# A new order of loads, and first weight products quarter by quarter, in a planned attention and feed-forward kernel

## The chip, the cores and the metric

The kernel runs on one core of a Trainium2 chip. The metric is the device time in microseconds (us) of one execution. Before the change the median of three runs is 355.5 us (355.44 to 355.51). The profiled execution took 354.98 us, and the instructions in its trace span 353.2 us; all moments below count from the start of that span.

## The reference

`q`, `k`, `v` have the shape (8 batches, 12 heads, 448 positions, 64). The reference computes

```python
q_n, k_n = rmsnorm(q, g_q), rmsnorm(k, g_k)
scores = q_n @ k_n.T / 8
attn = exp(scores - max); attn = attn / sum(attn)
x = (attn @ v)            # heads side by side: 3584 tokens x 768
a = x @ w1; b = x @ w2    # 768 -> 1024
out = ((a * b) @ w3) @ w_out   # 1024 -> 1024 -> 768
```

Inputs and output are float32.

## The kernel before, in words

**Tiling.** Attention is done in 24 "quads" of four heads each: quad `i` is batch `i // 3`, heads `4 * (i % 3)` onward. A quad needs its q and k (448 KB each in SBUF), a preparation (`plan_prep`: square on ACT, row sums on DVE, two short ACT instructions for the inverse root, scaling on DVE, then a transpose), seven score steps (`do_score`: four matmuls into two PSUM banks, then one exponential of 128x896 on ACT, 0.92 us), and the product of the exponentials with v (`do_pv_main`, `do_pv_rest`), which also sums them. Up to quad 4 (`N_PE_T = 5`) the transpose is done by TensorE (`do_turn`), later by a DMA. Two quads, when both are ready, go through the value product together: 72 long matmuls and 24 short ones.

**Weights.** Since nothing stands between `w3` and `w_out`, the kernel first makes their product `w34s`. For that, eight row blocks of `w3` (`load_w3`, called w0 to w7 in the load order) are turned over by TensorE (`do_w3_turn`, eight 128x128 transposes and a copy into `w3T`), and eight pairs of PSUM banks (`w34_pair`) each sum 64 matmuls over the eight row blocks of `w_out`, which come in four loads (`load_wout`, o0 to o3). `w1` and `w2` come in three loads each (a0 to a2, b0 to b2). Each batch then has eight `ffn1_pair`s (48 matmuls each: a, b and their product on DVE), and each two batches seven `ffn2_pair`s (64 matmuls each). These pairs of sums are the filler: TensorE works on them whenever no score or value product is ready.

**Halves of a pair.** A pair fills two banks. All contributions of one bank first come in one assignment of the array's row halves, then the halves change over. Before the change-over a "hand-over" instruction that does nothing (`hand_over`, L841) must pass on another queue, SyncE's until all of `w2` has landed and GpSimd's afterwards. `PARTS` says after which `w_out` row blocks the first three `w34_pair`s change over: `(4, 8)` means once in the middle of row blocks 0 to 3 and once in the middle of 4 to 7.

**The order of the work is planned in Python.** When the program is built, `Planner.run` plays the whole kernel through with fixed costs: each engine takes the job that can start first, and `pe_step` chooses TensorE's next piece. The instructions are written out in that order, and each engine's order is fixed from then on: an instruction whose data comes later than planned holds up all that stands behind it on its engine. The planner thinks of a load as an amount of work in a queue (the `moves` number, in us); two queues, SyncE's and GpSimd's, share the DMA engines, and a load lands `AFTER = 0.7` us after its last byte, and after 75 us of the plan `LATE` later still.

**What the names of the change mean.** `POOL_ORDER` is the order in which GpSimd issues its loads; `vN` and `qN` are v, and q with k, of quad N. `STOCK` and `PACE`: when at least `STOCK` feed-forward pairs wait, scores are started no closer than 1.7 us. `HOLD`: when set, a value product of two quads isn't started while pairs are unfinished and no waiting pair is ready. `quiet` in `plan_load_v`: from quad 4 on, the four v loads of a quad are issued only while less than `QUIET = 0.5` us of work is left in SyncE's queue. Where nothing else is ready in the first 13 us, TensorE is given matmuls on zeros (`do_warm`, L1182).

Of the kernel before, what the change touches and what calls it, by code (L numbers as in the profile page):

```python
# [19 lines left out]
INF = float("inf")  # L20
# [4 lines left out]
LAG = {"ACT": 0.11, "DVE": 0.09, "SP": 0.0, "POOL": 0.0}  # L25
AHEAD = {"SP": 2.0, "POOL": 1.6}
AFTER = 0.7
LATE = 1.0
BUSY = 75.0


# [14 lines left out]
class Planner:  # L46
# [11 lines left out]
    def add(self, *args, **kw):  # L58
        self.jobs.append(Job(*args, **kw))
# [37 lines left out]
    def commit(self, job, start, engine):  # L97
# [9 lines left out]
        if job.moves is not None:  # L107
# [4 lines left out]
            def landed(t):  # L112
                self.note(job, t, engine)
                t += LATE if t > BUSY else 0.0
                ticket[0] = t
# [80 lines left out]
def kernel(  # L196
# [48 lines left out]
    MARGIN = 0.25  # L245
    LOW = 2
    PV_BANKS = 6
    HOLD = 1
    SOON = 0
    STARVED = 4  # L250
    HUNGRY = 0.6
    ONE = 0
    PARTS = ((4, 8), (4, 8), (4, 8))
    EARLY_PAIRS = 3
    AHEAD_W3 = 4
    EARLY = 4
    STOCK = 18
    PACE = 1.7
    POOL_ORDER = (
        "w0 o0 o1 w1 w2 o2 o3 q1 v0 w3 w4 q2 v1 a0 w5 w6 a1 v2 w7 v3 q3 a2 q4 b0 b1 q5 b2".split()  # L260
    )
    ON_POOL = (1, 2, 3, 4, 5)
    IN_PARTS = (6, 7, 8)
    QUIET = 0.5

    w1s = const.tile([128, CM, DFF], BF, name="w1s")
# [47 lines left out]
    plan = Planner()  # L314
# [17 lines left out]
    w_at = {"w3": [INF] * CF, "w3T": [INF] * CF, "w_out": [INF] * 4, "w1": [INF] * NQB, "w2": [INF] * NQB}  # L332
# [6 lines left out]
    def all_of(times, n):  # L339
        return max(times) if len(times) == n else INF  # L340

    def put(where, key):
        def done(t):
            where[key] = t

        return done
# [23 lines left out]
    def plan_load_qk(i, key=None):  # L370
        eng, queue = (nc.gpsimd, "POOL") if i in ON_POOL else (nc.sync, "SP")
        parts = 2 if i in IN_PARTS else 1
        for which in range(2):
            got = []

            def done(t, which=which, got=got):
                got.append(t)
                landed[i]["qk"[which]] = all_of(got, parts)

            for n in range(parts):  # L380
                x0, x1 = 2 * n // parts, 2 * (n + 1) // parts
                add(
                    queue, {"SP": 0.4, "POOL": 0.75}[queue],
                    (QUAD * i - 30 if key is None else key) + which * 0.01 + n * 0.001,
                    lambda which=which, x0=x0, x1=x1: load_qk(i, which, eng, x0, x1),
                    needs=[lambda: qk_free[i % 3] + (1.0 if i > 5 else 0.0)],
                    done=done, moves=(1.4 / parts, 0.086),
                )

    def load_v(i, z):  # L390
# [15 lines left out]
    def plan_load_v(i, key):  # L406
        got = []

        def done(t):
            got.append(t)  # L410
            if len(got) == 4:
                landed[i]["v"] = max(got)

        def quiet():

            late = i <= 3 or next_score[0] >= i * NU - 3
            return 0.0 if late or sum(x[1] for x in plan.moving["SP"]) < QUIET else INF

        for z in range(4):
            add(  # L420
                "POOL", 0.62, key + z * 0.01, lambda z=z: load_v(i, z),
                needs=[lambda: v_free[i % 4] + (3.0 if i > 3 else 0.0), quiet], done=done,
                moves=((0.48, 0.06), (0.40, 0.05))[z % 2],
            )

    def load_w12(dst, src, m):
        return nc.gpsimd.dma_start(
            out=dst[:, 2 * m : 2 * m + 2, :].rearrange("p a f -> p (a f)"),
            in_=src.rearrange("(m p a) f -> m p (a f)", m=NQB, a=2)[m],
        )  # L430

    def load_w3(c):
        return nc.gpsimd.dma_start(
            out=w3s[:, c, :],
            in_=moe_w3.rearrange("(c p) f -> p c f", p=128)[:, c, :],
        )

    def load_wout(c):
        return nc.gpsimd.dma_start(
            out=w_outs[:, 2 * c : 2 * c + 2, :],  # L440
            in_=moe_w_out.rearrange("(c p) n -> p c n", p=128)[:, 2 * c : 2 * c + 2],
        )
# [194 lines left out]
    def score_ready(t):  # L637
# [6 lines left out]
        stock = sum(p.name != "w" for p in waiting)  # L644
        if stock >= STOCK and t < last_score[0] + PACE:
            return False
# [122 lines left out]
    def pv_summed(i, kind, z, end):  # L769
# [34 lines left out]
        if kind == 2:  # L804
            pv_end[i] = v_free[i % 4] = end + 0.2
            if i + 4 < NQ:
                plan_load_v(i + 4, -1.0)
# [85 lines left out]
    def w34_pair(fc):  # L893
        def evacuate(p, at):
# [23 lines left out]
            (side(0), side(1)), evacuate,  # L918
            PARTS[fc] if fc < len(PARTS) else None,
        )  # L920
# [309 lines left out]
    def pe_try(t, r):  # L1230
# [7 lines left out]
        if mode[0] == "v" and len(idle) >= 1 and size == 1:  # L1238
            return start_pv(t, 1, idle)
        last = HOLD and pairs and not any(p.ready() <= r for p in waiting)  # L1240
        if size == 2 and len(idle) >= PV_BANKS and not last:
# [45 lines left out]
    with tc.manual_schedule():  # L1287
        nc.vector.memset(warm_t, 0.0)
        nc.vector.memset(eps_t, 64e-6)
        nc.vector.memset(ones, 1.0)  # L1290
        nc.vector.memset(ones[HP:NP, 1], 0.0)
        nc.vector.memset(ones[0:HP, 2], 0.0)
        nc.vector.memset(ones_row, 1.0)
        for which in range(2):
            load_qk(0, which, nc.sync, 0, 1)
            load_qk(0, which, nc.scalar, 1, 2)
        nc.scalar.dma_start(out=g_row[:, 0], in_=g_q.unsqueeze(0))
        nc.scalar.dma_start(out=g_row[:, 1], in_=g_k.unsqueeze(0))
        nc.scalar.preload_act_table_set("natural_log_exp_and_others")
        make_identity(nc, ident)  # L1300
        for t_sb in v_bufs:
            nc.gpsimd.memset(t_sb[:, :, NF, :], 0.0)  # L1302
        def warm(n):
            for _ in range(n):
                nc.tensor.matmul(
                    out=ps_all[:, 7, :], lhsT=warm_t[:, 0:128], rhs=warm_t,
                    start=True, stop=True,
                )

        def g_product():  # L1310
            nc.vector.scalar_tensor_tensor(
                out=gp_row,
                in0=g_row[:, 0].unsqueeze(1).broadcast_to([1, 2, D]),
                scalar=8.0,
                in1=g_row[:, 1].unsqueeze(1).broadcast_to([1, 2, D]),
                op0=MULT, op1=MULT,
            )
            nc.tensor.matmul(
                out=ps_all[:, 6, 0:D], lhsT=ones_row, rhs=gp_row[:, 0],
                start=True, stop=True,  # L1320
            )
            nc.tensor.matmul(
                out=ps_all[:, 6, D : D + 1],
                lhsT=gp_row.rearrange("a x d -> a (x d)"), rhs=ones_row[:, 0:1],
                start=True, stop=True,
            )
            warm(1)

        def spread():
            nc.vector.tensor_copy(out=g_b, in_=ps_all[:, 6, 0:D])  # L1330
            nc.vector.tensor_copy(out=g_col, in_=ps_all[:, 6, D : D + 1])

        warm(WARM)
        free.update(ACT=4.0, DVE=4.0, SP=4.0, POOL=2.3, PE=7.2)
        plan.now = plan.moved_to = 2.2
        plan.moving["SP"].append([2.3, 2.6, lambda t: None, 0.086])
        landed[0].update(q=4.5, k=5.4)
        bank_at[6] = INF
        add(
            "DVE", 0.13, -13.0, g_product, needs=[lambda: 5.8], done=put(consts_at, "gp")  # L1340
        )
        add(
            "DVE", 0.22, -11.0, spread, needs=[lambda: consts_at["gp"] + 0.6],
            done=lambda t: consts_at.update(g=t + SEM) or bank_at.__setitem__(6, t + SEM),
        )
        for i in range(3):
            plan_prep(i)

        seq = [0]

        def weight(emit, moves, done):
            add("POOL", 0.6, -100.0 + seq[0], emit, done=done, moves=moves)

        for name in POOL_ORDER:
            what, x = name[0], int(name[1])
            seq[0] += 1
            if what == "o":
                weight(lambda x=x: load_wout(x), (2.15, 0.135), put(w_at["w_out"], x))
            elif what == "w":
                weight(lambda x=x: load_w3(x), (1.38, 0.172), put(w_at["w3"], x))  # L1360
            elif what == "v":
                plan_load_v(x, -100.0 + seq[0])
            elif what == "q":
                plan_load_qk(x, -100.0 + seq[0])
            else:
                dst, src, key = (w1s, moe_w1, "w1") if what == "a" else (w2s, moe_w2, "w2")
                weight(
                    lambda dst=dst, src=src, x=x: load_w12(dst, src, x), (2.6, 0.323),
                    put(w_at[key], x),
                )  # L1370
        waiting.extend(w34_pair(fc) for fc in range(CF))
        plan.run(pe_step, finished)
        if PLAN_OUT is not None:
            PLAN_OUT.append(dict(free))
# [28 lines left out]
```

## Time and profile before

| | |
|---|---|
| Time, median of 3 | 355.5 us |
| Span of the trace, granted clock of TensorE | 353.2 us, 1.000 |
| TensorE busy | 344.5 us (98%) |
| ScalarE (ACT) busy | 261.1 us (74%) |
| VectorE (DVE) busy | 206.5 us (58%) |
| DMA | 55.11 MB, mean 156 GB/s |
| Eighth and last `w3` block: issued, landed | 31.75, 38.94 us |
| First scores / first value product on TensorE | 12.18 / 24.23 us |
| End of the last matmul | 349.4 us |

"Busy" counts a matmul from its start to its modelled end. TensorE overlaps matmuls, so a short hole behind a group is counted as busy: a look at what the groups should take at their pace in a full stretch says more than the 98%. A time "landed" is the moment when the last of a load's sixteen parts was counted.

### The profile page before, as it was taken

To read this page: it belongs to the slowest core of one execution; us is meant where nothing else is said; L and a number is where in the kernel's file an instruction comes from. 1 tells how busy PE (TensorE), PEld (TensorE's weight loads), DVE (VectorE), ACT (ScalarE), POOL (GpSimd) and SP (SyncE) were. 2 spreads that over 40 slices of the span, in tenths; PEclk is the share of its full clock that TensorE was granted. 3 is DMA by queue.
4 is the path that set the end of the run, shared out by engine and by line. 5 is a ranking of instruction groups with operands and counts; after the bars stand their busy time and mean duration, and the time that the engine had idled before them with its cause. 6 is when DMAs were issued, how large, how long until landed. Compare 5 with 4: busy or idle time off the path is not lost.

```text
span 353.2 us, 16174 instructions
## 1 busy us (share of the span) xinstructions
PE 344.5 (98%) x7370; PEld 220.8 (63%) x7370; DVE 206.5 (58%) x292; ACT 261.1 (74%) x376; POOL 76.8 (22%) x134
## 2 busy tenths in 40 slices
PE   8899999999999999999999999999999999999995
PEld 4566756666665666667666565665656567666674
DVE  5359478897979487987767696576344320122200
ACT  5569979979989999999998999695979612222132
POOL 8365722211220403032032240230400000000000
PEclk9999999999999999999999999999999999999999
DMA  8999999598998999998999889783580005100046
GB/s 189 233 270 189 212 254 297 136 186 203 196 241 175 197 159 246 196 201 171 212 232 207 158 127 256 189 94 56 91 153 2 4 2 136 48 4 2 10 132 178
DMA packets 68488, 55.11 MB, mean 156 GB/s; under 512 B 45060, under 2 KB 62372, under 8 KB 68420
## 3 DMA queue, kind: packets, MB, share of 16 engines
q1 hardware_dynamic: 49440, 35.33, 44.7%
q0 software_dynamic: 18048, 16.92, 28.3%
q10 hardware_dynamic: 932, 1.84, 1.5%
q8 instruction: 57, 0.93, 1.1%
q14 instruction: 11, 0.09, 0.1%
HBM read 46.66 MB, written 11.01 MB: 163 GB/s over the span
## 4 chain that ended last, share of the span: by engine, by line
PE 87%; ACT 6%; DMA 2%; POOL 2%; issue 2%; DVE 1%; POOLq 0%; SPq 0%; ACTq 0%
PE ps_all L857 62%; PE ps_all L757 12%; PE ps_all L670 8%; ACT P L692 3%; PE ps_all L736 2%; DMA w_outs<-in_moe_w_out_dram 2%; ACT half L692 1%; POOL v_sb L399 1%; PE ps_all L1112 1%; PE ps_all L1053 1%; ACT Pr L692 1%; PE ps_all L1182 0%; DVE abT L938 0%; ACT qkT L350 0%; POOL v_sb L1302 0%
## 5 line engine op out<-in xcount | busy, mean ns | idle before, releaser
L692 ACT ACTIVATE P<-ps_all 128x896 bf16<-128x896 f32 x114 | 99.1, 922 | 9.7 <-PE ps_all L670 9.6
L399 POOL DMA_DIRECT2D v_sb<-in_v_dram x96 | 57.2, 609 | 176.8 <-PE ps_all L670 84.6
L857 PE MATMUL ps_all<-xT,w1s 64*64 64x448 bf16 x1536 | 89.4, 349 | 0.0
L857 PE MATMUL ps_all<-xT,w2s 64*64 64x448 bf16 x1536 | 88.0, 349 | 0.4 <-POOLq L841 0.4
L857 PE MATMUL ps_all<-w34s,abT 64*64 64x384 bf16 x1728 | 80.5, 323 | 0.1
L350 ACT ACTIVATE half<-ps_all 128x896 bf16<-128x896 f32 (+1 forms) x40 | 34.8, 869 | 56.1 <-PE ps_all L857 56.1
L938 DVE TENSOR_TENSOR abT<-ps_all,half 128x896 bf16<-128x896 f32 x32 | 34.8, 1089 | 57.3 <-PE ps_all L857 56.8
L857 PEld LDWEIGHTS <-abT 64*64 64x64 bf16 x1728 | 52.2, 107 | 19.6 <-POOLq L841 0.5
L857 PEld LDWEIGHTS <-w2s 64*64 64x64 bf16 x1536 | 47.6, 107 | 25.3 <-POOLq L841 0.8
L857 PEld LDWEIGHTS <-w1s 64*64 64x64 bf16 x1536 | 46.1, 107 | 25.5 <-issue 0.2
L670 PE MATMUL ps_all<-qkT 64*64 64x448 bf16 x672 | 60.9, 352 | 0.9 <-ACT P L692 0.4
L462 DVE TENSOR_REDUCE ssq<-sq 128x14 f32<-128x896 f32 (+1 forms) x50 | 51.2, 1041 | 13.9 <-ACT sq L455 13.9
L485 DVE TENSOR_TENSOR qks<-qk_sb,al 128x448 bf16<-128x448 f32 x96 | 55.5, 617 | 1.4 <-ACT al L474 1.1
L455 ACT ACTIVATE sq<-qk_sb 128x896 f32<-128x896 f32 (+1 forms) x50 | 45.3, 917 | 1.6 <-DMA qk_sb<-in_q_dram 1.5
L799 DVE TENSOR_TENSOR xT<-ps_all,r 128x448 bf16<-128x448 f32 x48 | 27.4, 617 | 12.7 <-ACT r L780 10.1
L670 PEld LDWEIGHTS <-qkT 64*64 64x64 bf16 x672 | 21.7, 106 | 14.9 <-issue 5.1
L857 PE MATMUL ps_all<-w_outs,w3T 64*64 64x384 bf16 x512 | 24.9, 324 | 1.6 <-DMA w_outs<-in_moe_w_out_dram 1.0
L692 ACT ACTIVATE w_outs<-ps_all 128x896 bf16<-128x896 f32 x24 | 21.5, 915 | 5.3 <-PE ps_all L670 5.1
L757 PE MATMUL ps_all<-P,v_sb 128*32 128x448 bf16 x456 | 25.0, 352 | 0.0
L692 ACT ACTIVATE Pr<-ps_all 128x896 bf16<-128x896 f32 x24 | 22.3, 929 | 1.7 <-PE ps_all L670 1.6
L757 PEld LDWEIGHTS <-v_sb 128*32 128x32 bf16 x592 | 15.8, 97 | 12.2
L356 DVE COPY half<-ps_all 128x768 f32<-128x768 f32 x9 | 8.6, 956 | 22.0 <-PE ps_all L857 14.0
(66 smaller groups left out, 214.8 us busy)
## 6 DMA issues: line engine op xcount, KB each, us to landing
out_dram<-half SPq DMA_DIRECT2D x48, 192.0 KB, 3.5
qk_sb<-in_q_dram SPq DMA_DIRECT2D x15, 448.0 KB, 5.3
qk_sb<-in_k_dram SPq DMA_DIRECT2D x15, 448.0 KB, 5.8
v_sb<-in_v_dram POOLq DMA_DIRECT2D x48, 64.0 KB, 3.9
v_sb<-in_v_dram POOLq DMA_DIRECT2D x48, 48.0 KB, 4.2
qk_sb<-in_q_dram POOLq DMA_DIRECT2D x5, 448.0 KB, 8.3
qk_sb<-in_k_dram POOLq DMA_DIRECT2D x5, 448.0 KB, 10.1
w3s<-in_moe_w_dram POOLq DMA_DIRECT2D x8, 256.0 KB, 7.5
```

Of the source, the lines that this page charges most:

```text
L350: nc.scalar.activation(out=out, in_=in_, func=AF.Copy, scale=1.0 if by is None else by)
L356: nc.vector.tensor_copy(out=out, in_=in_)
L399: nc.gpsimd.dma_start(out=v_bufs[i % 4][p0 : p0 + HP, g::2, 0 : j1 - j0].rearrange("p h j d -> p h (j d)"), in_=src[:, g::2, j0:j1].rearra ...
L455: nc.scalar.activation(out=s["sq", t][:, x0:x1], in_=src[:, t, x0:x1], func=AF.Square)
L462: nc.vector.tensor_reduce(out=s["ssq"][:, t, x0:x1], in_=s["sq", t][:, x0:x1], axis=AX, op=ADD)
L485: nc.vector.tensor_tensor(out=s["qks"][:, t, :, x], in0=src[:, t, x], in1=s["alpha"][:, t, x].unsqueeze(2).broadcast_to([NP, NJ, D]), op=MULT,
L670: nc.tensor.matmul(out=sc[HP * c : HP * c + HP, u, 0:S].rearrange("p (j s) -> p j s", j=NJ), lhsT=qkT[u * D : (u + 1) * D, 1, j, cols], rh ...
L692: lambda: nc.scalar.activation(out=dst, in_=sc[:, :, 0:S], func=AF.Exp),
L757: nc.tensor.matmul(out=ps_all[hd * HALF : (hd + 1) * HALF, z, 0:S], lhsT=value_weights(i, hd, j, kind), rhs=s["P"][:, hd, j, :] if j < NF ...
L799: lambda: nc.vector.tensor_tensor(out=xT[b][:, 2 * m + kind - 1, :], in0=ps, in1=s["r"], op=MULT),
L857: mm = nc.tensor.matmul(out=ps_all[64 * h : 64 * h + 64, p.bank + z, 0 : p.n], lhsT=lhsT[64 * r : 64 * r + 64, 64 * h : 64 * h + 64], rhs= ...
L938: nc.vector.tensor_tensor(out=abT[bp][:, f0 : f0 + 2, odd * S : (odd + 1) * S], in0=ps_all[:, z : z + 2, 0:S], in1=a_sb[b, f0], op=MULT,)
```

## The change

The loads from GpSimd are put into a new order: o0 goes ahead of w0, the first three w blocks follow, and o1 to o3 come after them; further on v1, v2 and v3 are set between the big weight loads, and b0 and b1 go ahead of q4. The first two `w34_pair`s change over four times, quarter by quarter, so that each needs only o0 for its first sixteen matmuls. The planner's costs of the loads are set to measured landing times: 1.95 for 2.15 (o), 1.27 for 1.38 (w), 2.7 for 2.6 (a, b), 1.35 for 1.4 (q, k), 0.46 and 0.38 for 0.48 and 0.40 (v), and 3.5 for 2.6 for quad 0's own q and k at the start. `LATE` falls from 1.0 to 0.3. Two choices of the planner change: `HOLD` is off and `STOCK` is 14. `quiet` now looks at both queues.

```diff
-LATE = 1.0
+LATE = 0.3
...
-    HOLD = 1
+    HOLD = 0
...
-    PARTS = ((4, 8), (4, 8), (4, 8))
+    PARTS = ((2, 4, 6, 8), (2, 4, 6, 8), (4, 8))
...
-    STOCK = 18
+    STOCK = 14
     PACE = 1.7
     POOL_ORDER = (
-        "w0 o0 o1 w1 w2 o2 o3 q1 v0 w3 w4 q2 v1 a0 w5 w6 a1 v2 w7 v3 q3 a2 q4 b0 b1 q5 b2".split()
+        "o0 w0 w1 w2 o1 o2 o3 q1 v0 w3 w4 q2 w5 a0 v1 w6 w7 v2 a1 v3 q3 a2 b0 b1 q4 q5 b2".split()
     )
...
+    FIRST = 3.5
...
-                    done=done, moves=(1.4 / parts, 0.086),
+                    done=done, moves=(1.35 / parts, 0.086),
...
-            return 0.0 if late or sum(x[1] for x in plan.moving["SP"]) < QUIET else INF
+            left = [sum(x[1] for x in plan.moving[e]) for e in ("SP", "POOL")]
+            return 0.0 if late or max(left) < QUIET else INF
...
-                moves=((0.48, 0.06), (0.40, 0.05))[z % 2],
+                moves=((0.46, 0.06), (0.38, 0.05))[z % 2],
...
-        plan.moving["SP"].append([2.3, 2.6, lambda t: None, 0.086])
+        plan.moving["SP"].append([2.3, FIRST, lambda t: None, 0.086])
...
-                weight(lambda x=x: load_wout(x), (2.15, 0.135), put(w_at["w_out"], x))
+                weight(lambda x=x: load_wout(x), (1.95, 0.135), put(w_at["w_out"], x))
...
-                weight(lambda x=x: load_w3(x), (1.38, 0.172), put(w_at["w3"], x))
+                weight(lambda x=x: load_w3(x), (1.27, 0.172), put(w_at["w3"], x))
...
-                    lambda dst=dst, src=src, x=x: load_w12(dst, src, x), (2.6, 0.323),
+                    lambda dst=dst, src=src, x=x: load_w12(dst, src, x), (2.7, 0.323),
```

## The prediction, on record before the run

> **What bounds the kernel now.** I read the page's busy line first, then who TensorE waited for, then the chain that ended last, then the timeline of the first 25 us.
>
> ```profile
> PE 344.5 (98%) x7370; PEld 220.8 (63%) x7370; DVE 206.5 (58%) x292; ACT 261.1 (74%) x376; POOL 76.8 (22%) x134
> ```
> ```profile
> PE ps_all L857 <- DMA w_outs<-in_moe_w_out_dram: 1.0, 1, 1.0
> PE ps_all L670 <- ACT P L692: 0.4, 2, 0.2
> ...
> PE ps_all L857 <- ACT P L692: 0.4, 1, 0.4
> PE ps_all L736 <- ACT w34s L350: 0.4, 1, 0.4
> ```
> ```profile
> 2.94 7.15 DMA w_outs<-in_moe_w_out_dram
> ...
> 32.21 1.30 PE ps_all L857 x32
> ...
> 93.61 4.73 PE ps_all L857 x100
> ```
> ```profile
> 7.65 1.04 PE L1182 MATMUL ps_all<-warm_t 128*128 128x256 bf16 x8
> 8.56 0.56 PE L1112 MATMUL ps_all<-ident,qks 128*128 128x128 bf16 x7
> 10.14 0.52 PE L857 MATMUL ps_all<-w_outs,w3T 64*64 64x384 bf16 x8 [1.01 <-DMA w_outs<-in_moe_w_out_dram]
> 10.59 0.39 PE L1182 MATMUL ps_all<-warm_t 128*128 128x256 bf16 x2
> 10.82 0.55 PE L1112 MATMUL ps_all<-ident,qks 128*128 128x128 bf16 x7
> 11.21 1.04 PE L1182 MATMUL ps_all<-warm_t 128*128 128x256 bf16 x8
> 12.18 0.57 PE L670 MATMUL ps_all<-qkT 64*64 64x448 bf16 x8
> ...
> 17.65 6.64 PE L857 MATMUL ps_all<-w_outs,w3T 64*64 64x384 bf16 x144
> 24.23 0.75 PE L757 MATMUL ps_all<-P,ones 128*32 128x448 bf16 x12
> ```
>
> TensorE is the bound: the other engines have a quarter or more free. The chain gives its pace in full stretches: 0.0406 us for a matmul of 384 columns (32 in 1.30), 0.0473 for one of 448 (100 in 4.73); 14 transposes take 0.89, so 0.064 each. At these prices: 3072 feed-forward matmuls of 448 columns 145.3 us, 2240 of 384 columns 91.0, 672 for scores 31.8, 888 for values 42.0, 264 short ones 6.6 (0.2 for eight), 134 transposes 8.6, and the last tile 2.8. That is **328.1 us of work that no reordering removes**, so 25.1 of the 353.2 are lost. Setting the matmul starts against these prices, stretch by stretch, puts the losses at: 0 to 10 us 9.0; 10 to 20 us 2.8; 20 to 40 us 0.8; 40 to 50 us 0.8; 50 to 350 us about 8, no ten us of it over 1.1 (110 to 120 us; then 0.6 each at 200 to 220) but for the end; after the last matmul about 4. Most of the first 9 is quad 0's loading and preparation, which the change leaves alone. The prize is what lies between 9 and 50 us, 4 to 5 us in all.
>
> The timeline shows the mistake there. Eight products for `w34s` stand in TensorE's queue at 9.1 us and wait 1.01 us for o0; behind them the seven transposes of quad 0's k, ready at about 9.6, start only at 10.8; so quad 0's scores start at 12.18.
>
> **What the Trainium skill says.** "DMA: Bandwidth & Descriptors", section "Issuing engines are not separate DMA queues": all DMAs end up on the same 16 engines and interleave, whoever issued them. The trace agrees: GpSimd's first fifteen loads land one after another, 1.22 to 1.28 us apart for a w, 1.86 to 1.89 for an o, so a new order moves no byte sooner in total. The same page, "Latency and other measured facts", says engines 7 and 15 are usually slower than the rest. The trace doesn't name engines, but of o0's sixteen parts fourteen landed by 8.87, the last two at 9.70 and 10.09, and that lag stays about the same through o3. So a load is counted with its slowest part, and I take landings from the sixteenth. The same page's "Rules for kernel authors" advises to issue a load early and to wait late; this kernel's planner does that, as far as its landing times are right.
>
> **The change part by part.**
>
> *New places at the start.* Landings before: w0 6.97, o0 10.09, o1 11.98, w1 13.23, w2 14.51, o2 16.37, o3 18.26. The new queue has o0 first, and after w0 the same 640 KB have passed, so w0 lands at about 10.1 (if the late pair of parts is tied to o0 and not to the moment: 9.0; I take 10.1). Then w1 +1.26 = 11.35, w2 12.6, o1 14.5, o2 16.4, o3 18.3.
>
> *TensorE to the first scores.* The built order of the new kernel has, after the last 512-column warm matmul (6.98): 13 warm matmuls, 7 transposes of q, 7 warm, 7 of k, turn of w0, 2 warm, turn of w1, then 8 score matmuls. A warm one takes 0.11 (8 from 7.65 to the next start at 8.56). Start 7.2 + 13 x 0.11 = 8.6 for q as before; k at 9.1 + 0.75 = 9.85 instead of 10.82; turn 0 at 10.3; turn 1 waits for w1 at 11.35 and ends at 11.9; k's copy (0.63) is long done. So scores start at 11.9, not 12.18, and TensorE has then done 30 transposes, 1.9 us, where before it had 1.8 (22 transposes and 8 products). That is **-0.5 us** with the 0.28 of the earlier start; between -1.1 (turn 1 not held) and 0 (w1 0.5 later).
>
> *From the first scores to the first value product.* Before, 12.18 to 24.23 is 12.05 us with 9.9 of work, 2.15 lost: waits for exponentials at 14.4, 15.2 and 16.8 and hand-overs (the L841 rows before 19.57, 21.85 and 23.45). The quarters let three pairs offer 48 products (1.95 us) on o0 alone, where `(4, 8)` offers 24, so there is something between any two scores; the built order has 12 or 16 products there. The score pace stays at the exponential's 0.83 to 0.92, so a part of the holes stays. I put the loss at 1.6: **-0.5** (bounds -1.0 and +0.3). No load binds: v0 landed at 21.96, and the product would start at about 11.9 + 9.7 + 1.6 = 23.2. The four more hand-overs wait 0.4 to 0.5 each as those seen; SyncE has nothing else queued until 52 us, and the other two pairs run in the gap. I count them in the 1.6.
>
> *Quad 1.* Its k landed at 21.00 and was scaled by 26.8, for which ACT and DVE are the reason (the square of k at 21.85, behind a `w34s` copy). The new ACT order still has a `w34s` copy before those squares. A TensorE that comes 1.0 earlier waits there for k: **+0.4** (0 to +0.9).
>
> *Filler ahead of quads 1 and 2.* At 44.72 the value product waits for ACT, and 44 to 46 us loses 0.6. The old order leaves one `w34_pair` (64 products, 2.6 us) for after it; the new one finishes all eight before, with 88 products in a row directly ahead. That covers the wait: **-0.5** (-0.6 to 0). This comes through the new places of w5 to w7 and the new costs.
>
> *Small v loads among the weights, b0 and b1 ahead of q4.* The loads up to a2 are the same set, so a2 lands at about 47 as before; the first product with w1 comes near 50. b2 stays last at about 61.6; the new order does all four w1 pairs of batch 0 first and comes to w2 near 62. q4 comes 5 us later, at about 54, and its transposes stand near 61. All hidden: 0, with little to spare for b2 (0 to +0.5).
>
> *`LATE`, `STOCK`, `HOLD`, both queues in `quiet`, smaller costs.* With 0.7 us less reserve, a square may stand ahead of its load on ACT. Before, the square began this long after its q had landed: at least 3 us for most quads, but 0.13, 0.75, 0.74 and 0.02 for quads 15, 18, 20 and 22. If each of those four is placed 0.7 earlier, ACT waits 0.6 + 0 + 0 + 0.7 = 1.3 us, of which TensorE with its filler should feel less than half: +0.4 (0 to +1.3). Against it, fewer scores in a burst: near 117 us the old order has 16 score matmuls with nothing between them, the new one 12, in the stretch that loses 1.1; and v loads that are spaced out leave GpSimd free for hand-overs (0.40 lost at 207): -0.5 (-1.0 to 0). Scores end later in the order, but the end is still over 55 us of plain feed-forward work. Net **-0.1**.
>
> Sum: -0.5 - 0.5 + 0.4 - 0.5 - 0.1 = -1.2; **355.5 - 1.2 = 354.3 us**.
>
> **The rivals.** *Bigger gain, 353.2*: w1 doesn't hold up turn 1 (-0.6 more), quad 1 isn't late and its +0.4 falls away. For it: ACT and DVE are idle for 1 to 4 us at times before 23 us. Against: k1 cannot land earlier.
> *No change to be measured, 355.3*: TensorE comes earlier to quad 1 and to later value products, which are set by q and k landings and by ACT, and waits there. For it: the chain runs through ACT for 5 us at 38 to 43. Against: filler is in the order at just that place.
> *Slower, 356.4*: two or three early squares or missing weights hold a queue. The early gain of 1.0 and the 0.5 at 44 us are outweighed by 1.3 on ACT carried whole to TensorE, 0.5 at b2, and 0.6 at new places where a pair or a v load is planned too tightly. For it: reserve is taken from every load while DMA is busy up to 230 us (tenths of 8 and 9 in the page's slices). Against: most squares have 3 us of slack.
>
> **How the numbers follow.** Forecast case 0.42, bigger gain 0.16, no change 0.23, slower 0.19. Faster by over 0.2% (0.7 us) has the first two: 0.58; within 0.23; slower 0.19. The single bounds would add to about 352.3 and 357.5, but they don't all fall one way; 352.9 to 356.0 leaves out the far part of the slower case (0.13) and a little of the bigger gain (0.05).
>
> **What would show it.** In the changed profile: no wait for `w_outs` at 10 us; k's transposes near 9.9; a wait of TensorE for w3 at 10 to 12 us; scores at 11.9; the first value product near 23.2; no wait at 46 us before the value product of quads 1 and 2. The forecast is wrong if waits of ACT's squares for q or k loads grow beyond 1.5 us and TensorE's waits for exponentials with them, or if the hand-overs of the quarters take more than 1.6 us from TensorE before 24 us.

## The result, and the profile after

The changed kernel takes 353.93 us (median of 6, 353.51 to 354.39) against 355.5 us (median of 6) for the kernel before on the same chip: a ratio of 0.995, 95% interval 0.9937 to 0.9963. It is **faster by 0.5%, 1.6 us**; the forecast was 354.3. The profiled execution spans 352.1 us, where the one before spans 353.2; that one took 354.98 us in all, half a us under its kernel's median, so the profiles differ by less than the medians.

The busy line, TensorE's whole list of waits and the start of the timeline, to be held against those of before:

```profile
PE 344.4 (98%) x7374; PEld 227.7 (65%) x7374; DVE 208.8 (59%) x295; ACT 260.3 (74%) x373; POOL 76.6 (22%) x134
```
```profile
PE ps_all L1307 <- DVE warm_t L1290: 1.2, 1, 1.2
PE ps_all L759 <- issue: 0.5, 2, 0.3
PE ps_all L859 <- DVE w3T L357: 0.5, 1, 0.5
PE ps_all L672 <- ACT Pr L694: 0.4, 1, 0.4
PE ps_all L859 <- DVE xT L801: 0.2, 1, 0.2
PE ps_all L859 <- issue: 0.2, 1, 0.2
```
```profile
9.01 0.93 PE L1184 MATMUL ps_all<-warm_t 128*128 128x256 bf16 x7
9.78 0.55 PE L1114 MATMUL ps_all<-ident,qks 128*128 128x128 bf16 x7
10.16 0.61 PE L1136 MATMUL ps_all<-ident,w3s 128*128 128x128 bf16 x8
10.61 0.38 PE L1184 MATMUL ps_all<-warm_t 128*128 128x256 bf16 x2
10.83 0.61 PE L1136 MATMUL ps_all<-ident,w3s 128*128 128x128 bf16 x8
11.37 0.57 PE L672 MATMUL ps_all<-qkT 64*64 64x448 bf16 x8
...
16.34 5.87 PE L859 MATMUL ps_all<-w_outs,w3T 64*64 64x384 bf16 x128
22.14 0.75 PE L759 MATMUL ps_all<-P,ones 128*32 128x448 bf16 x12
```

("issue" is idle time for which the profile shows no wait.) The wait for `w_outs` is gone, k's transposes run at 9.78 instead of 10.82, the scores start at 11.37 instead of 12.18 and the first value product at 22.14 instead of 24.23: 2.1 us won by then. But the spans differ by 1.1 only. The busy shares say nothing of this; TensorE is at 98% in both. What tells is the same account as in the prediction, each matmul at its pace in a full stretch and the rest counted as lost. Lost until the given moment, us:

| | 30 | 50 | 100 | 250 | 340 |
|---|---|---|---|---|---|
| before | 12.7 | 13.4 | 14.8 | 19.7 | 20.5 |
| changed | 10.9 | 11.9 | 12.5 | 18.6 | 19.5 |
| lead | 1.8 | 1.5 | 2.3 | 1.1 | 1.0 |

**In these two profiles the gain is made before 30 us, and half of it is given back between 100 and 250 us.** Of the 1.2 us given back, some 0.7 are on balance "issue" gaps: two of those in the list above, at 174.25 and 220.92 us, cost 0.5 and 0.6 us by this account, and one in the kernel before, at 216.72 us, costs 0.4. The experiments ask what made it and what took it back.

### The profile page after: what moved, and what is told of

The parts are those of the page before. It is cut to its first block, busy times and chain, and to the rows that moved or that the text cites. A ratio compares the mean times of both kernels' runs of the same rounds, so it can differ in the third digit from the quotient of the medians.

```text
span 352.1 us, 16194 instructions
## 1 busy us (share of the span) xinstructions
PE 344.4 (98%) x7374; PEld 227.7 (65%) x7374; DVE 208.8 (59%) x295; ACT 260.3 (74%) x373; POOL 76.6 (22%) x134
## 4 chain that ended last, share of the span: by engine, by line
PE 93%; DVE 3%; ACT 2%; issue 1%; POOLq 0%; DVEq 0%
PE ps_all L859 66%; PE ps_all L759 11%; PE ps_all L672 9%; PE ps_all L738 2%; PE ps_all L1307 2%; ACT P L694 2%; PE ps_all L1114 1%; DVE qks L487 1%; PE ps_all L1055 1%; PE ps_all L1184 1%; PE ps_all L1136 1%; DVE xT L801 1%; DVE ssq L464 0%; DVE w34s L357 0%; ACT Pr L694 0%
## 5 line engine op out<-in xcount | busy, mean ns | idle before, releaser
L694 ACT ACTIVATE P<-ps_all 128x896 bf16<-128x896 f32 x114 | 99.6, 923 | 11.3 <-PE ps_all L672 11.1
L859 PE MATMUL ps_all<-xT,w2s 64*64 64x448 bf16 x1536 | 89.6, 349 | 0.3 <-DVE xT L801 0.2
L351 ACT ACTIVATE half<-ps_all 128x896 bf16<-128x896 f32 (+1 forms) x36 | 31.5, 876 | 49.5 <-PE ps_all L859 49.3
L859 PEld LDWEIGHTS <-abT 64*64 64x64 bf16 x1728 | 55.1, 107 | 17.7 <-issue 1.2
L859 PEld LDWEIGHTS <-w2s 64*64 64x64 bf16 x1536 | 49.6, 107 | 24.3 <-issue 0.8
L859 PEld LDWEIGHTS <-w1s 64*64 64x64 bf16 x1536 | 48.6, 107 | 24.3 <-POOLq L843 0.9
L672 PE MATMUL ps_all<-qkT 64*64 64x448 bf16 x672 | 62.3, 352 | 0.4 <-ACT Pr L694 0.4
L672 PEld LDWEIGHTS <-qkT 64*64 64x64 bf16 x672 | 23.1, 106 | 12.8 <-issue 4.6
L694 ACT ACTIVATE w_outs<-ps_all 128x896 bf16<-128x896 f32 x24 | 21.5, 913 | 4.6 <-PE ps_all L672 4.4
L759 PEld LDWEIGHTS <-v_sb 128*32 128x32 bf16 x592 | 16.0, 97 | 13.4 <-issue 1.6
L694 ACT ACTIVATE Pr<-ps_all 128x896 bf16<-128x896 f32 x24 | 22.1, 922 | 1.1 <-PE ps_all L672 1.1
L357 DVE COPY half<-ps_all 128x768 f32<-128x768 f32 x13 | 12.4, 955 | 14.4 <-PE ps_all L859 13.7
## 6 DMA issues: line engine op xcount, KB each, us to landing
qk_sb<-in_k_dram POOLq DMA_DIRECT2D x5, 448.0 KB, 12.4
```

Source lines behind the costliest of these rows:

```text
L351: nc.scalar.activation(out=out, in_=in_, func=AF.Copy, scale=1.0 if by is None else by)
L357: nc.vector.tensor_copy(out=out, in_=in_)
L672: nc.tensor.matmul(out=sc[HP * c : HP * c + HP, u, 0:S].rearrange("p (j s) -> p j s", j=NJ), lhsT=qkT[u * D : (u + 1) * D, 1, j, cols], rh ...
L694: lambda: nc.scalar.activation(out=dst, in_=sc[:, :, 0:S], func=AF.Exp),
L759: nc.tensor.matmul(out=ps_all[hd * HALF : (hd + 1) * HALF, z, 0:S], lhsT=value_weights(i, hd, j, kind), rhs=s["P"][:, hd, j, :] if j < NF ...
L859: mm = nc.tensor.matmul(out=ps_all[64 * h : 64 * h + 64, p.bank + z, 0 : p.n], lhsT=lhsT[64 * r : 64 * r + 64, 64 * h : 64 * h + 64], rhs= ...
```

## The experiments

All times are compared with the kernel before, run beside them on the same chip; that kernel came to 355.5 to 356.1 us there, so the ratio, not the time, is what is compared between experiments. The changed kernel has 0.995. A profile shows one execution, and it can lie well off the median, as in experiments 2 and 3. Diffs against the changed kernel say so; the others are against the kernel before.

**1. The start alone: order, quarters and costs.** LATE, STOCK, HOLD and the quiet rule stay as before.

```diff
-    PARTS = ((4, 8), (4, 8), (4, 8))
+    PARTS = ((2, 4, 6, 8), (2, 4, 6, 8), (4, 8))
...
-        "w0 o0 o1 w1 w2 o2 o3 q1 v0 ...
+        "o0 w0 w1 w2 o1 o2 o3 q1 v0 ...
...
-                weight(lambda x=x: load_wout(x), (2.15, 0.135), put(w_at["w_out"], x))
+                weight(lambda x=x: load_wout(x), (1.95, 0.135), put(w_at["w_out"], x))
```

> The kernel before with the new order of loads, the quarters and the new costs of loads; LATE, HOLD, STOCK and the wait for a quiet queue as before. Theory: the change wins some 2.2 us before 24 us and gives about 1 us back after 100 us, because LATE of 0.3 sets squares on ACT ahead of loads that land later. Then this kernel keeps the first value product near 22.1 us, and comes to 353.0 us (352.6 to 353.5). Rival: STOCK, HOLD and the two queues in the quiet rule carry part of the gain; then this one comes to 354.5 to 355.

Measured: 354.43 us, ratio 0.9979 (0.9957 to 1.0002). The first value product came at 22.51 with the last warm matmul 0.6 later than in the changed kernel, so the start is all there, and the lead at 30 us is 1.4 (11.3 lost). By 250 us it is gone: 19.8 lost, as before the change (19.7). So the expectation of 353.0 failed, and the time is close to the rival's: with the old `LATE` the early gain is given back too, in this profile all of it.

**2. `LATE` back at 1.0**, against the changed kernel.

```diff
-LATE = 0.3
+LATE = 1.0
```

> The changed kernel with LATE back at 1.0 and nothing else undone; its plan is the same for the first 75 us. Theory: ACT's waits for q and k loads after 75 us fall from 3.3 us to under 1, the 0.7 us that TensorE loses at 150 us is gone, 353.2 us. Rival: those waits are only a sign of TensorE being earlier everywhere, and cost nothing; 353.9 us as the changed kernel, or more.

Measured: 353.68 us, ratio 0.9947 (0.9928 to 0.9966), as the changed kernel. ACT's waits for q and k loads are nearly gone (3.8 us in the changed kernel, 0.9 here), yet the time is the same. The waits were as foreseen; that they alone decide the time is not so. Where this plan loses instead is not shown: its profile is of the slowest of 14 executions (355.51 us), and loses 1.1 us at 146 to 148 in the middle of a run of matmuls, in a gap for which the profile shows no wait.

**3. Halves in place of quarters**, against the changed kernel.

```diff
-    PARTS = ((2, 4, 6, 8), (2, 4, 6, 8), (4, 8))
+    PARTS = ((4, 8), (4, 8), (4, 8))
```

> The changed kernel with the halves (4, 8) in place of the quarters. Theory: the gain at the start is that no product stands ahead of its load; the quarters add little: scores at 11.4 us as in the changed kernel, first value product at 22.1 to 22.6, 353.9 to 354.4 us. Rival: the quarters are what fills the time between the first scores; first value product at 23.5 or later, about 355 us.

Measured: 356.99 us, ratio 1.004 (1.002 to 1.0061): slower than before the change. TensorE's timeline of this kernel, from the first scores on:

```profile
11.80 0.57 PE L672 MATMUL ps_all<-qkT 64*64 64x448 bf16 x8
12.20 0.49 PE L859 MATMUL ps_all<-w_outs,w3T 64*64 64x384 bf16 x8
12.63 0.62 PE L1136 MATMUL ps_all<-ident,w3s 128*128 128x128 bf16 x8
13.20 0.38 PE L672 MATMUL ps_all<-qkT 64*64 64x448 bf16 x4
14.01 0.52 PE L859 MATMUL ps_all<-w_outs,w3T 64*64 64x384 bf16 x8 [0.42 <-DVE w3T L357]
...
18.49 5.34 PE L859 MATMUL ps_all<-w_outs,w3T 64*64 64x384 bf16 x112 [0.61 <-DMA w_outs<-in_moe_w_out_dram]
23.76 0.75 PE L759 MATMUL ps_all<-P,ones 128*32 128x448 bf16 x12
```

The scores are as early, but the halves leave nothing to do at 13.6 and run out of `w_outs` at 17.9. The value product comes 11.96 us after the first scores; in the changed kernel it is 10.77 (22.14 less 11.37). So in these two profiles the quarters save about 1.2 us by there; the rival was right on this. The profile is of one of the slowest executions (359.86 us, 2.9 over the median). At its end it has 5 us more lost than the one before (25.5 at 340 us), most of it far from the start: 2.4 at 30 to 50, where the changed kernel loses 1.0 (1.4 of the 2.4 is an "issue" gap at 45.1), and 2.4 at 220 to 240, where ACT's squares of the last quads wait for their loads.

**4. The order alone.**

```diff
-        "w0 o0 o1 w1 w2 o2 o3 q1 v0 w3 w4 q2 v1 a0 w5 w6 a1 v2 w7 v3 q3 a2 q4 b0 b1 q5 b2".split()
+        "o0 w0 w1 w2 o1 o2 o3 q1 v0 w3 w4 q2 w5 a0 v1 w6 w7 v2 a1 v3 q3 a2 b0 b1 q4 q5 b2".split()
```

> The kernel before with the new order of loads alone. Theory: the order pays only with landing times that are right; with the old ones the plan still expects o0 and w0 at other moments than they come, and half the gain at the start is lost: first value product near 23.3, 354.8 us. Rival: the order alone does it, 354.0 us or less. Second rival: the built order alone makes it slower, over 356 us.

Measured: 355.13 us, ratio 0.9985 (0.9966 to 1.0003). The first scores came at 11.52 and the first value product at 22.49, so the start is early here too; by 50 us little of it is left (12.7 lost, 13.4 before). A small gain or none.

**5. Order and costs, without the quarters.**

```diff
-        "w0 o0 o1 w1 w2 ...
+        "o0 w0 w1 w2 o1 ...
...
-                weight(lambda x=x: load_w3(x), (1.38, 0.172), put(w_at["w3"], x))
+                weight(lambda x=x: load_w3(x), (1.27, 0.172), put(w_at["w3"], x))
```

> The kernel before with the new order of loads and the new costs, halves (4, 8) kept, LATE, HOLD, STOCK and the quiet rule as before: the quarters are all that stands between this and the first experiment. Theory after four runs: the quarters are worth about 1 us by the first value product (23.3 us without them, 22.1 with them, on the same start), and carry it to the end: 355.2 us against 354.4 with them. Rival: the third experiment was slow only through its late squares, and quarters are worth nothing: 354.4.

Measured: 356.83 us, ratio 1.002 (1.0003 to 1.0036). The first value product came at 23.13, 11.60 after the first scores; with the quarters (first experiment) 10.59. Here the two built orders are the same up to 13.3 us, so this pair is the cleanest: **the quarters are worth 1.0 us at the start** in it. Over all profiles with the new order and costs, seven with quarters need 10.59 to 11.38 us from the first scores to the first value product, 10.95 on the mean, and two with halves (experiments 3 and 5) 11.96 and 11.60: some 0.8 us. They are not the only way there: the halves of experiment 4, in the order that the old costs give, need 10.97, though that kernel then loses 1.3 us up to 30 us, where the changed one loses 0.5. The ratios differ by 0.4% at the end; after experiment 12 that can't be put down to the quarters.

**6. The quarters alone.**

```diff
-    PARTS = ((4, 8), (4, 8), (4, 8))
+    PARTS = ((2, 4, 6, 8), (2, 4, 6, 8), (4, 8))
```

> The kernel before with the quarters alone. Theory: eight products still stand ahead of k's transposes and wait for o0 until 10.1 us, so the scores start at 12.2 as before; the quarters save 0.5 at most: 355.3 us, no clear change. Rival: quarters alone carry the gain: 354.3 us.

Measured: 358.7 us, ratio 1.0073 (1.0045 to 1.01): slower, which no theory had. The scores start at 12.20, as expected, and the first value product comes 11.45 us after them, 0.6 sooner than in the two profiles of the old start with halves (12.05 before, 12.11 in experiment 7); but the halves of experiment 12, on another plan, also need 11.45. The loss is 2.5 us at 30 to 50 and 2.9 at 50 to 100, where the kernel before loses 0.7 and 1.4, long after the quarters are done.

**7. The later choices alone.**

```diff
-LATE = 1.0
+LATE = 0.3
...
-    HOLD = 1
+    HOLD = 0
...
-    STOCK = 18
+    STOCK = 14
...
-            return 0.0 if late or sum(x[1] for x in plan.moving["SP"]) < QUIET else INF
+            left = [sum(x[1] for x in plan.moving[e]) for e in ("SP", "POOL")]
+            return 0.0 if late or max(left) < QUIET else INF
```

> The kernel before with LATE 0.3, STOCK 14, HOLD 0 and both queues in the quiet rule, and with the old order, quarters and costs: the start is as before. Theory: the gain is at the start, and these choices alone win nothing: 355.8 us. Rival: they are worth the 1 us by which the changed kernel beats the first experiment: 354.8 us.

Measured: 356.34 us, ratio 1.0007 (0.9985 to 1.003): no change. More telling is its start, which in the built order is exactly that of the kernel before:

```profile
8.62 0.55 PE L1113 MATMUL ps_all<-ident,qks 128*128 128x128 bf16 x7
9.16 0.52 PE L858 MATMUL ps_all<-w_outs,w3T 64*64 64x384 bf16 x8
9.62 0.39 PE L1183 MATMUL ps_all<-warm_t 128*128 128x256 bf16 x2
9.85 0.55 PE L1113 MATMUL ps_all<-ident,qks 128*128 128x128 bf16 x7
10.26 1.03 PE L1183 MATMUL ps_all<-warm_t 128*128 128x256 bf16 x8
11.22 0.57 PE L671 MATMUL ps_all<-qkT 64*64 64x448 bf16 x8
```

No wait for o0, and scores at 11.22. In this execution o0's last part landed at 9.12, in that of before at 10.09. **The wait of 1.01 us on which the prediction's first step stands is there in some executions only** (0.52 us in the sixth experiment, none in the seventh, under 0.1 in the twelfth).

**8. `STOCK` back at 18**, against the changed kernel.

```diff
-    STOCK = 14
+    STOCK = 18
```

> The changed kernel with STOCK back at 18. Theory: the start is the same, scores come in tighter bursts again and ACT has less room after a late load: 354.3 us, 0.4 slower than the changed kernel. Rival: STOCK has no effect on the end: 353.9 us.

Measured: 354.07 us, ratio 0.9936 (0.9904 to 0.9969): no difference from the changed kernel that can be told. The rival holds.

**9. Shorter q and k loads from quad 9 on**, against the changed kernel; every engine's order is the same. The kernel leaves out the rest of these loads.

```diff
+        n = NJ * D if i < 9 else 4 * D
...
-            out=qk_bufs[i % 3][:, which, x0:x1].rearrange("p x j d -> p x (j d)"),
-            in_=src.rearrange("(x g) (p j) d -> (g p) x (j d)", x=2, j=NJ)[:, x0:x1],
+            out=qk_bufs[i % 3][:, which, x0:x1].rearrange("p x j d -> p x (j d)")[:, :, 0:n],
+            in_=src.rearrange("(x g) (p j) d -> (g p) x (j d)", x=2, j=NJ)[:, x0:x1, 0:n],
```

> The changed kernel, every instruction in its place, but the loads of q and k from quad 9 on bring only 4 of 7 columns of rows, so they land earlier; the rest of these quads works on what lay there (part of the computation is left out). If the early gain is given back after 75 us because squares stand ahead of their loads: ACT's waits for q and k loads after 75 us (3.3 us) go to nearly 0, and the time falls by 0.7 to 1.2 us, to a ratio of 0.992 of the kernel before. If the loads are not what gives it back: ratio 0.995 as the changed kernel.

Measured: 352.15 us, ratio 0.991 (0.9892 to 0.9929), and 17.2 us lost by 250 us against 18.6. ACT's waits for q and k loads fall from

```profile
ACT sq L457 <- DMA qk_sb<-in_k_dram: 2.1, 3, 1.1
...
ACT sq L457 <- DMA qk_sb<-in_q_dram: 1.7, 2, 1.2
```

to a single one:

```profile
ACT sq L458 <- DMA qk_sb<-in_q_dram: 0.5, 1, 0.5
```

That is the remaining wait in the first 75 us. Since no instruction moved, this gain of some 0.4% belongs to the loads. It needn't all come through ACT's waits: there is less to move for every other load too, and the gap at 220.92 is not in this profile. Nor is it shown that the change brought all of this cost, since no run shortened the loads of the kernel before; its ACT has a single such line, of which 0.3 us fall after 60 us (3.3 in the changed kernel):

```profile
ACT sq L455 <- DMA qk_sb<-in_q_dram: 1.5, 3, 0.7
```

How a late load reaches TensorE can be read in the changed kernel's timeline at 148 us, all engines, rows picked in order of time:

```profile
148.08 0.95 ACT L457 ACTIVATE sq<-qk_sb 128x896 f32<-128x896 f32 x1 [0.69 <-DMA qk_sb<-in_k_dram]
...
149.07 1.09 DVE L464 TENSOR_REDUCE ssq<-sq 128x14 f32<-128x896 f32 x1 [0.56 <-ACT sq L457]
...
150.07 0.62 DVE L487 TENSOR_TENSOR qks<-qk_sb,al 128x448 bf16<-128x448 f32 x1
...
150.60 0.62 DVE L801 TENSOR_TENSOR xT<-ps_all,r 128x448 bf16<-128x448 f32 x1
...
152.34 0.95 PE L859 MATMUL ps_all<-xT,w2s 64*64 64x448 bf16 x16 [0.22 <-DVE xT L801]
```

Quad 15's k lands at 148.00. Its square has been at the head of ACT's queue for 0.69 us; the row sums and the scaling follow late on DVE, and the `xT` product, which had nothing to do with quad 15, stands behind the scaling. TensorE runs out of feed-forward matmuls before `xT` is there: 0.7 us lost at 150 to 160. In the ninth experiment the two squares run back to back at 146.42 (one row of two, 1.78 us), and 150 to 160 us lose 0.2.

**10. Shorter squares from quad 9 on**, against the changed kernel; TensorE's and GpSimd's orders are the same. The kernel leaves out most of each square, and the squares lie in three fixed buffers.

```diff
+    sq_bufs = [const.tile([NP, 2, NJ, D], FP, name="sq" + str(z)) for z in range(3)]
...
-                s["sq", t] = prep_pool.tile([NP, 2, NJ, D], FP, tag="sq", name="sq")
+                s["sq", t] = sq_bufs[(2 * i + t) % 3]
+            n = NJ if i < 9 else 2
             nc.scalar.activation(
-                out=s["sq", t][:, x0:x1], in_=src[:, t, x0:x1], func=AF.Square
+                out=s["sq", t][:, x0:x1, 0:n], in_=src[:, t, x0:x1, 0:n], func=AF.Square
             )
```

> The changed kernel with TensorE's and GpSimd's order untouched, but the squares from quad 9 on take only 2 of 7 columns (part of the computation is left out): ACT has some 0.6 us less to do for each of 30 squares. If ACT, busy for 90 to 95 of 100 us until 230 us, is what takes the gain back, TensorE's losses between 100 and 250 us (6.3 us) fall by 2 or more and the ratio comes to 0.990. If TensorE's order alone sets the pace: 0.995, and ACT waits for TensorE instead.

Measured: 353.51 us, ratio 0.9943 (0.9916 to 0.997): not to be told from the changed kernel. ACT's waits for TensorE's scores grow from 11.1 to 16.8 us (L694, here L696), so the time that it saves it waits. Its profile loses 17.5 us by 250 us, 1.1 less than the changed kernel's, but the median doesn't confirm a gain of that size. The 0.990 expected if ACT's work gives the lead back lies outside the interval; a smaller share isn't ruled out.

**11. `LATE` at 1.0 and `STOCK` at 18**, against the changed kernel. `HOLD` makes no difference in any engine's built order, with or without the start, so beside the first experiment only the quiet rule is left.

```diff
-LATE = 0.3
+LATE = 1.0
...
-    STOCK = 14
+    STOCK = 18
```

> The changed kernel with LATE at 1.0 and STOCK at 18: what is left beside the first experiment is the quiet rule with both queues (HOLD makes no difference to the built order). If the quiet rule carries the 0.3% by which the changed kernel beats the first experiment: ratio 0.994. If LATE or STOCK carry it: 0.998. The fourth case, each of the three replans the later part with a different luck: anything between 0.992 and 1.0, not to be told apart.

Measured: 353.44 us, ratio 0.9941 (0.9918 to 0.9965). The quiet rule on both queues is all that stands between this and the first experiment's 0.9979; the intervals touch. Neither `LATE` nor `STOCK` is needed for the gain. One place can be read: in the first experiment's profile a hand-over waits on GpSimd behind v loads,

```profile
201.93 1.33 PE L857 MATMUL ps_all<-xT,w2s 64*64 64x448 bf16 x24 [0.54 <-POOLq L841]
```

and TensorE loses 0.8 us there by the account. Of the six profiles with the old rule, five have such a wait at 202 to 209 us (0.6 to 0.8 lost); none of the eight with the new rule has one there. The four plans that share the new start, the quarters and the new rule (the changed kernel, experiments 2, 8 and 11) come to 0.9936 to 0.995, so the gain as a whole does not hang on one lucky plan.

**12. The kernel before, planned with another margin.**

```diff
-    MARGIN = 0.25
+    MARGIN = 0.24
```

> The kernel before with the planner's MARGIN at 0.24 for 0.25, a change that means nothing by itself; TensorE's order differs from the first scores on. If the plan is stable: within 0.1% of the kernel before. If replanning alone moves the time: over 0.2% to either side, and then a single choice of the later part can't be credited with a difference of that size.

Measured: 358.25 us, ratio 1.008 (1.006 to 1.0099). A change of 0.01 us in the time for which work must have been ready to be taken first makes the kernel **2.7 us slower**. It loses what the quarters alone lose, and at the same places:

| lost by, us | 30 | 50 | 100 | 250 | 340 |
|---|---|---|---|---|---|
| before | 12.7 | 13.4 | 14.8 | 19.7 | 20.5 |
| quarters alone (6) | 12.4 | 14.9 | 17.8 | 23.0 | 23.7 |
| margin 0.24 (12) | 11.8 | 14.2 | 17.0 | 22.6 | 23.5 |
| changed | 10.9 | 11.9 | 12.5 | 18.6 | 19.5 |
| short loads (9) | 10.9 | 11.3 | 12.5 | 17.2 | 18.0 |

So replanning by itself can move the time by more than the change under study does. The end times of the experiments that replan (1 to 8 and 11) show what that plan costs, not what the edited number is worth; the start, before the plans part, and the experiments that keep the order (9 and 10) can be read as cause and effect.

## Why the prediction was right

The direction, the size (-1.2 us forecast, -1.6 measured) and the place of the gain were right. Several of its terms were not, and that the sum fits is partly luck: in the two profiles the terms up to the first value product were too small by 1.1 us and the later choices too favourable by 1.3, which cancels.

*To the first scores, -0.5 forecast.* The mechanism is as written, with k's transposes at 9.78 (9.85 forecast) and no products ahead of them. Turn 1 was not held by w1: w1 landed at 10.31 instead of 11.35. I had carried the late pair of parts over to the new queue; in this execution o0's sixteen parts lie within 6.98 and 7.81. So scores came at 11.37, not 11.9. In the seven kernels with this start they came between 11.31 and 11.92. But with the old order and an o0 that wasn't late, experiment 7 had them at 11.22: the term is real only in executions where o0 is late.

*To the first value product, -0.5 forecast.* It was more: in the two profiles 1.3 us (the lead goes from 0.8 to 2.1), over the seven profiles of the new start 1.1 on the mean (10.95 against 12.05 and 12.11), 0.2 of it because the turn of w1 now comes ahead of the scores. The quarters do fill the time (experiments 1 and 5), with fewer products than the prediction counts: the third pair still has halves, so the three offer 16 + 16 + 8 = 40 on o0 alone, not 48. But part of the 2.1 is an unlucky execution of before: with the same start the seventh experiment reached its value product at 23.33, not 24.23. The seven kernels with the new start lie between 22.11 and 23.09. Between these and the two of the old start lie 1.3 us on the mean (22.4 against 23.8).

*Quad 1, +0.4 forecast.* The amount was about right, the cause not: k's transposes found their data at 25.37. TensorE waits 0.51 us at 26.88 for a copy of a turned `w3` block, as in the list of waits.

*Before the value product of quads 1 and 2, -0.5 forecast.* The wait at 44.7 is gone. The changed kernel's profile loses 0.7 us at 48 to 50 instead, partly in an "issue" gap (0.26 before a value matmul at 48.63), and next to nothing from 50 to 60. Over 40 to 60 us it loses 0.9 where the kernel before loses 1.4, and experiments 8 to 10, with the same order there, lose 0.7 to 0.9. The gain is the forecast's.

*Small v loads, b0 and b1, 0 forecast.* TensorE's list shows no wait for `w1s` or `w2s`.

*Later choices, -0.1 forecast.* This is the term that was mis-sized: in the profile, 1.2 us of the lead go between 100 and 250 us. The part of the loads is at the edge of its bounds (0 to +1.3): experiment 9 puts it at about 0.4%, 1.4 us, for all q and k loads from quad 9 on. The prediction looked at q alone; of the 3.3 us that ACT waits after 60 us, 2.1 are for the k of quads 15, 16 and 22. Of the two things said to offset it, fewer scores in a burst at 117 us didn't: 110 to 120 us loses 1.1 as before. The hand-over at 207 us did come free, and 200 to 220 us loses 0.2 where it lost 1.2; but three other hand-overs now wait on GpSimd, at 104, 111 and 146 us, for 1.1 us in all by the account. And `LATE` isn't the sole lever: undone, it takes the waits away, and the time stays (experiment 2). What stays open is which of the replanned places costs the other kernels their lead, and what the "issue" gaps are; after experiment 12 I would not put it down to a single number of the planner.

Of what the prediction named as signs of being wrong, one half came true: ACT's waits for q and k loads grew from 1.5 to 3.8 us. TensorE's waits for exponentials, which were to grow with them, fell from 1.4 to 0.4.

The rival "slower" named the true danger, squares ahead of loads, and overrated it. Half of "bigger gain" came true: w1 didn't hold up the turn, but quad 1 was late. "No change" failed; of its two reasons, the loads of q and k do take something back (experiment 9), and ACT, given less to do, mostly waits longer (experiment 10).

## What to carry to other kernels

In a kernel whose order is fixed by a plan, an instruction placed ahead of a load that comes late holds up all that stands behind it, also work that has nothing to do with that load; look for the first waits for DMA on every engine, not on the bound engine alone. Cutting the first products so that each needs only the first piece of a weight is a gain that can be checked at one place in the timeline (0.8 to 1.0 us here). And before a gain of half a per cent is credited to a tuned number, change one that means nothing: here 0.01 us of margin moved the time by 0.8%.

## What the runs showed of the hardware

The same loads, issued at the same moments, don't land at the same moments: o0, second in the old queue and issued at 2.94 or 2.95, landed at 10.09, 10.00, 9.12 and 9.22 us in four executions. In the first two, fourteen of the sixteen parts were in by 8.9 and two came 0.7 to 1.2 us later. The Trainium skill ("DMA: Bandwidth & Descriptors", section "Latency and other measured facts") has two engines that are usually slower; here two parts are late in some executions and in others not, and no trace names the engines. So a plan with landing times to the hundredth of a us is still off by up to a whole one.

The matmuls on zeros at the start took different times: the first of the 512-column ones started at 1.19 us in every profile, the fifteenth between 5.58 and 7.08 us, with nothing changed in between. A start that ends 0.5 us earlier in one profile than in another is no sign of a better kernel.
